# Loading the decay vector by rows and starting the r and k loads behind it: the prologue of a recurrent-attention plus ELU feed-forward kernel

## The chip, the cores and the metric

The kernel runs on one core of one Trainium2 chip. The metric is device time in microseconds (us) of one execution; lower is better. A profile of one execution on the same chip shows what each engine did. The engines are TensorE (PE, its weight loads PEld), VectorE (DVE), ScalarE (ACT), GpSimd (POOL), and SyncE (SP), which issues nearly all loads.

## The reference

Inputs are `r`, `k`, `v` of shape (4, 8, 768, 48) (batch B, heads H, steps S, head size D), the decay `w` and the bonus `u` of shape (8, 48), and two weight matrices of 384x2048 and 2048x384. All are float32.

```python
def _attn_ref(r, k, v, w, u):
    state = np.zeros((B, H, D, D)); y = np.zeros_like(r)
    for t in range(S):
        kt, vt, rt = k[:, :, t], v[:, :, t], r[:, :, t]
        cur = np.einsum('bhd,bhe->bhde', u[None] * kt, vt)
        y[:, :, t] = np.einsum('bhd,bhde->bhe', rt, state + cur)
        state = w[None, :, :, None] * state + np.einsum('bhd,bhe->bhde', kt, vt)
    return y

def _moe_ref(x, w_in, w_out):
    h = x @ w_in
    g = np.where(h > 0.0, h, np.exp(np.minimum(h, 0.0)) - 1.0)
    return g @ w_out
```

The attention output, turned to (3072, 384), goes through the feed-forward layer.

## The kernel before

The 768 steps are cut into six chunks of 128; a unit is one chunk of one batch, so there are 24 units. In a unit, r and k are turned by TensorE (products with the identity, `turn_in`, written `Tr` and `Tk` in the order), scaled by powers of w (`decay_r`, `decay_k`: `dr`, `dk`), multiplied with each other (`scores`: `A`), masked, and multiplied with v. The feed-forward weights are split into a high and a low part, and each layer product is made of three products. In the steady part TensorE goes through hidden and output products of 16 slices of the feed-forward layer per chunk, with the attention of later units put between.

The powers of w are good in this form only when every w lies between 0.8 and 1.2. So the program makes a flag, every engine reads it (`values_load`, L1122) and branches (`tc.If`, L1123) either to the fast path (`arm(general=False)`, the one that runs with these inputs) or to a general one. What comes ahead of the branch is `prepare` (L82 to L160).

In `prepare`, SP issues, in this order: w as one row of 384 on one partition (L89, for the test), w by channels into `w_col` (L94, two transfers in which every element lies by itself in memory), r of unit 0, u, k of unit 0, r and k of unit 1, v of unit 0. DVE takes minimum and maximum of the row (L122, L123) and makes the flag (L124, L126), and scans `w_col` four times to make the table of powers `pw` (L145). POOL makes the identity, clears the unused columns of the r, k and v tiles (`clear_pads`, L159), makes the mask and clears the states. PE runs seven float32 products of the identity with itself that nobody reads (`warm`, L497); each is two passes. `prepare` is written without an order: a scheduler puts each engine's instructions in a row.

Behind the branch the order is written out by hand (`tc.manual_schedule`), each engine going through it in its own program order. It begins `jk:8 inv Tr:0 dr:0 ub rua:0 rub:0 Lrk:2 Tk:0 ...`: eight more unread products with the identity (`keep_warm`, L502), the table of inverse powers on DVE (`inv`, L514 to L518), Tr and dr of unit 0 (L610, L670), u spread over the partitions (`ub`, a PE product at L506 and an ACT copy at L507), the products of r, k and u on POOL (`rua`, `rub`), the loads of unit 2, and Tk of unit 0. `Lw` are loads of feed-forward weights (L218, L221), `Lnk:0` (L171) the loads of r and k for the second chunk of batch 0.

Of the kernel before, what the change touches and what calls it, by code (L numbers as in the profile page):

```python
# [8 lines left out]
F32 = mybir.dt.float32  # L9
# [6 lines left out]
ALU = mybir.AluOpType  # L16
AX = mybir.AxisListType
PSUM = bass.MemoryType.PSUM

P = 128  # L20
B, H, S, D = 4, 8, 768, 48
DP = 64
HP = H // 2
DM, DFF = 384, 2048
# [6 lines left out]
ROWS = [slice(i * DP, i * DP + D) for i in range(2)]  # L31
# [1 line left out]
FILL = DP - D  # L33
Q = P // HP
W_LOW, W_HIGH = 0.8, 1.2
WARM = 7

DEEP, WIDE = 3, 2

START = """  # L40
jk:8 inv Tr:0 dr:0 ub rua:0 rub:0 Lrk:2 Tk:0 rua:1 rub:1 dk:0 sum:0 vd:0 Tr:1 zw dr:1 pr A:0 m0:0 Tk:1 Lrk:3 PT Lv:1
Tr:2 dk:1 kr:0 A:1 sum:1 m1:0 Lw:0 dr:2 Tk:2 d0a:1 m0:1 Y:0 ru:2 dk:2 Lv:2 Tk:3 d1a:1 m1:1 Tr:3 ru:3 xh:0 Y:1 sum:2
d1a:2 wd:0 xh:1 xl:0 dk:3 dr:3 kr:1 sum:3 d0:3 ma:0 Lw:3 Lw:4 A:2 d0a:2 xl:1 d1:3 S:0 sp:0 m1:2 Lv:3 m0:2 A:3 Lw:2
Lw:1 wd:2 S:1 m0:3 Y:2 Lnk:0 m1:3 rsd:0 xh:2 Lw:6 Y:3 xh:3 ma:2 sp:2 H:0 wdi:1 xl:2
# [28 lines left out]
class Kernel:  # L73
# [7 lines left out]
    def prepare(self, ctx):  # L81
        nc, tc = self.nc, self.tc  # L82
        cp = ctx.enter_context(tc.tile_pool(name="cp", bufs=1))

        self.rev = cp.tile([P, H, DP], F32, tag="rev", name="rev")
        self.state = [cp.tile([P, HP, 2 * D], F32, tag=f"state{b}", name=f"state{b}") for b in range(B)]
        early = self.rev.rearrange("p h d -> p (h d)")
        w_row = early[0:1, 0:DM]
        nc.sync.dma_start(w_row, self.w.rearrange("(o h) d -> o (h d)", o=1))  # L89

        w_col = cp.tile([P, HP], F32, tag="w_col", name="w_col")
        nc.vector.memset(w_col, 1.0)
        for i, rows in enumerate(ROWS):
            nc.sync.dma_start(w_col[rows, :], self.w[i::2, :].rearrange("a d -> d a"))  # L94

        self.slots = [
            (
                cp.tile([P, H, DP], F32, tag=f"r_t{i}", name=f"r_t{i}"),
                cp.tile([P, H, DP], F32, tag=f"k_t{i}", name=f"k_t{i}"),
                cp.tile([P, H, DP], F32, tag=f"v_t{i}", name=f"v_t{i}"),  # L100
            )
            for i in range(2)
        ]
        self.ident = cp.tile([P, P], F32, tag="ident", name="ident")
        make_identity(nc, self.ident)
        ones = early[:, DM:]
        nc.vector.memset(ones, 1.0)
        self.raw = {}
        for b in range(2):
            self.raw[0, b] = self.slots[b]  # L110
            self.clear_pads(self.slots[b])
        self.load_rk(0, 0, (0,))
        self.u_b = cp.tile([P, H, D], F32, tag="u_b", name="u_b")
        self.u_row, self.one = early[DP : DP + 1, 0:DM], ones[DP : DP + 1, :]
        nc.sync.dma_start(self.u_row, self.u.rearrange("(o h) d -> o (h d)", o=1))
        self.load_rk(0, 0, (1,))
        self.load_rk(0, 1)
        self.load_v(0, 0)


        lim = cp.tile([1, 4], F32, tag="lim", name="lim")
        nc.vector.tensor_reduce(lim[:, 0:1], w_row, axis=AX.X, op=ALU.min)  # L122
        nc.vector.tensor_reduce(lim[:, 1:2], w_row, axis=AX.X, op=ALU.max)  # L123
        nc.vector.tensor_single_scalar(out=lim[:, 2:3], in_=lim[:, 0:1], scalar=W_LOW, op=ALU.is_ge)  # L124
        self.flag = cp.tile([1, 1], I32, tag="flag", name="flag")
        nc.vector.scalar_tensor_tensor(  # L126
            self.flag, lim[:, 1:2], W_HIGH, lim[:, 2:3], op0=ALU.is_le, op1=ALU.mult
        )

        self.warm(WARM)  # L130


        self.mask = cp.tile([P, P], F32, tag="mask", name="mask")
        nc.gpsimd.memset(self.mask, 1.0)
        nc.gpsimd.affine_select(
            out=self.mask, in_=self.mask, pattern=[[1, P]], compare_op=ALU.is_gt,
            fill=0.0, base=0, channel_multiplier=-1,
        )
        for t in self.state:
            nc.gpsimd.memset(t, 0.0)  # L140
        self.pw = cp.tile([P, HP, P + 1], F32, tag="pw", name="pw")
        nc.vector.memset(self.pw[:, :, 0:1], 1.0)

        for a in range(HP):
            nc.vector.tensor_tensor_scan(  # L145
                self.pw[:, a, 1 : P + 1], w_col[:, a : a + 1].to_broadcast([P, P]), ones,
                1.0, op0=ALU.mult, op1=ALU.mult,
            )

        self.pairs = []  # L150
        for k in range(NF + 1):
            self.pairs.append([
                cp.tile([P, self.count(k), DM], F32R, tag=f"{n}{k}", name=f"{n}{k}")
                for n in ("wh", "wl")
            ])
# [333 lines left out]
                    self.done.add((name, m, b))  # L489
                    units[name](m, b)  # L490

    def warm(self, times):

        with self.tc.tile_pool(name="ps_w", bufs=1, space=PSUM) as ps:
            junk = ps.tile([P, P], F32, tag="junk", name="junk")
            for _ in range(times):
                self.nc.tensor.matmul(junk, lhsT=self.ident, rhs=self.ident, start=True, stop=True)  # L497

    def keep_warm(self, times):
        junk = self.ps.tile([P, T], F32, tag="h", name="junk", bufs=2)  # L500
# [615 lines left out]
@with_exitstack  # L1116
def rwkv_elu_ffn(ctx: ExitStack, tc: tile.TileContext, r, k, v, w, u, w_in, w_out, out):
    nc = tc.nc
    kn = Kernel(tc, r, k, v, w, u, w_in, w_out, out)
    kn.prepare(ctx)  # L1120

    near_one = nc.values_load(kn.flag, min_val=0, max_val=1)  # L1122
    with tc.If(near_one > 0) as cmp:  # L1123
        kn.arm(general=False)
    with cmp.Else():
        kn.arm(general=True)
# [30 lines left out]
```

## Time and profile before

| what | value |
|---|---|
| median of 3 runs | 495.19 us (494.24, 495.19, 496.57) |
| the profiled execution: its own time | 494.27 us |
| its span, first to last instruction | 492.5 us |
| PE busy | 483.7 us (98%) |
| DVE busy | 300.2 us (61%) |
| ACT busy | 244.6 us (50%) |
| POOL busy | 124.7 us (25%) |
| bytes moved by DMA | 49.13 MB |

Busy time counts instructions that compute; the unread products of the prologue count too. The end of a PE instruction is modelled, so rows of PE overlap a little. The 1.77 us between the execution's own time and its span lie outside the first and the last instruction.

### The profile page before, as it was taken

Reading aid. Unit: us, or ns where it says so; the run is one execution under the profiler, and the core shown is the slowest. Engines: PE = TensorE matmul, PEld = TensorE weight load, DVE = VectorE, ACT = ScalarE, POOL = GpSimd, SP = SyncE. Lnnn points to the kernel's source line nnn. Section 1 sums busy time; section 2 is a strip of 40 time slices with the busy share of each in tenths; the row PEclk is TensorE's granted clock in tenths of the full one; section 3 lists DMA queues with packets and bytes.
Section 4 is the critical chain, followed back from the end, with each engine's and each line's share of the span. In section 5 each row is a group of like instructions: output and inputs, shape, how many; then the busy total and the mean of one; then the engine's idle time right before and its main releaser. Section 6 shows DMA issues by size and latency. Waiting matters only on the chain.

```text
span 492.5 us, 12293 instructions
## 1 busy us (share of the span) xinstructions
PE 483.7 (98%) x5085; PEld 402.1 (82%) x5085; DVE 300.2 (61%) x514; ACT 244.6 (50%) x477; POOL 124.7 (25%) x156
## 2 busy tenths in 40 slices
PE   8999999999999999999999999999999999999995
PEld 7877887888888888888888888888888878889995
DVE  6989898955577647657457656475674443433332
ACT  3887776544435543544535435435444353344341
POOL 7766456451133231131220321301111000000000
PEclk9999999999999999999999999999999999999999
DMA  8899887561545461462431625514532000010002
GB/s 139 223 229 235 171 215 205 151 132 52 136 87 135 97 136 44 119 145 61 103 106 41 144 67 112 136 45 92 126 68 85 11 1 0 10 33 23 2 1 71
DMA packets 108454, 49.13 MB, mean 100 GB/s; under 512 B 89442, under 2 KB 104292, under 8 KB 108388
## 3 DMA queue, kind: packets, MB, share of 16 engines
q1 hardware_dynamic: 96580, 43.91, 39.1%
q10 hardware_dynamic: 11808, 4.33, 3.8%
q8 instruction: 42, 0.69, 0.6%
q14 instruction: 24, 0.20, 0.2%
HBM read 35.12 MB, written 13.11 MB: 98 GB/s over the span
## 4 chain that ended last, share of the span: by engine, by line
PE 85%; DVE 4%; DMA 3%; SPq 3%; ACT 2%; issue 1%; DVEq 0%; ACTq 0%
PE ps_acc L1080 38%; PE ps_h L1028 36%; PE ps_a L777 4%; PE ps_y L810 3%; DMA stage<-in_moe_w_in_dram 1%; PE ps_y L797 1%; DMA k_t<-in_k_dram 1%; SPq L171 1%; SPq L218 1%; PE ps_y L921 1%; PE ps_y L792 1%; DVE stage L562 1%; DMA stage<-in_moe_w_out_dram 1%; DVE wl L599 1%; DVE ps_h L1043 1%
## 5 line engine op out<-in xcount | busy, mean ns | idle before, releaser
L1028 PE MATMUL ps_h<-x,wh 128*128 128x512 f32 (+1 forms) x582 | 192.6, 388 | 0.9 <-DVE g L1051 0.6
L1080 PE MATMUL ps_acc<-g,wh 128*128 128x512 f32 x480 | 163.5, 396 | 0.1
L1043 DVE SCALAR_TENSOR_TENSOR ps_h<-g,ps_h 128x512 f32<-128x512 f32 x96 | 66.6, 694 | 126.0 <-ACT g L1038 125.9
L1028 PEld LDWEIGHTS ps_h<-x,wh 128*128 128x128 f32 x582 | 108.8, 188 | 24.7 <-DVE g L1051 1.8
L1037 ACT ACTIVATE g<-ps_h 128x512 f32<-128x512 f32 x96 | 57.3, 597 | 127.5 <-PE ps_h L1028 99.6
L1028 PE MATMUL ps_h<-x,wl 128*128 128x512 f32 (+1 forms) x291 | 112.7, 387 | 0.0
L1080 PEld LDWEIGHTS ps_acc<-g,wh 128*128 128x128 f32 x480 | 90.0, 188 | 20.9 <-issue 0.8
L1080 PE MATMUL ps_acc<-g,wl 128*128 128x512 f32 x240 | 93.7, 390 | 0.0
L1049 ACT ACTIVATE g<-ps_h 128x512 fp32r<-128x512 f32 x96 | 57.3, 597 | 70.0 <-DVE ps_h L1043 59.2
L1051 DVE SCALAR_TENSOR_TENSOR g<-ps_h,g 128x512 fp32r<-128x512 f32 x96 | 66.2, 690 | 41.8 <-ACT g L1049 37.2
L1028 PEld LDWEIGHTS ps_h<-x,wl 128*128 128x128 f32 x291 | 54.6, 188 | 10.9
L828 POOL TENSOR_TENSOR a<-ident,diag 128x512 f32<-128x512 f32 x22 | 24.3, 1106 | 152.3 <-PE ps_y L921 79.8
L1038 ACT ACTIVATE g<-g 128x512 f32<-128x512 f32 x96 | 60.7, 632 | 3.1
L1080 PEld LDWEIGHTS ps_acc<-g,wl 128*128 128x128 f32 x240 | 45.1, 188 | 8.7
L658 POOL TENSOR_TENSOR tb<-rk,qw 128x512 f32<-128x512 f32 x16 | 20.8, 1301 | 69.6 <-DMA rk<-blocks 69.6
L1080 PE MATMUL ps_acc<-wh,g 128*128 128x384 f32 x128 | 33.9, 336 | 0.0
L835 DVE COPY_PREDICATED a<-mask,ps_a 128x512 f32<-128x512 int32 x46 | 33.4, 734 | 0.2 <-ACT a L824 0.2
L824 ACT ACTIVATE a<-ident,diag 128x128 f32<-128x128 f32 x96 | 30.4, 391 | 0.4 <-DVE diag L715 0.4
L1080 PEld LDWEIGHTS ps_acc<-wh,g 128*128 128x128 f32 x128 | 23.2, 188 | 0.4 <-DVE g L1051 0.2
L946 ACT CAST x<-ps_y 128x256 fp32r<-128x256 f32 (+1 forms) x40 | 10.8, 322 | 22.8 <-DVE state L936 21.0
L1080 PE MATMUL ps_acc<-wl,g 128*128 128x384 f32 x64 | 21.4, 335 | 0.0
L732 POOL TENSOR_TENSOR sw<-state,pw 48x192 f32<-48x192 f32 x30 | 18.2, 607 | 7.4 <-DVE state L936 6.3
(111 smaller groups left out, 442.6 us busy)
## 6 DMA issues: line engine op xcount, KB each, us to landing
blocks<-tb SPq DMA_DIRECT2D x64, 128.0 KB, 2.4
rk<-blocks SPq DMA_DIRECT2D x16, 512.0 KB, 3.5
stage<-in_moe_w_out_dram SPq DMA_DIRECT2D x16, 383.8 KB, 4.6
stage<-in_moe_w_in_dram SPq DMA_DIRECT2D x64, 95.8 KB, 3.9
out_dram<-stage ACTq DMA_DIRECT2D x80, 48.0 KB, 1.7
r_t<-in_r_dram SPq DMA_DIRECT2D x17, 192.0 KB, 4.4
k_t<-in_k_dram SPq DMA_DIRECT2D x17, 192.0 KB, 5.0
v_t<-in_v_dram SPq DMA_DIRECT2D x17, 192.0 KB, 5.4
```

The costliest lines, as they stand in the source:

```text
L658: (self.nc.gpsimd if i else self.nc.vector).tensor_mul(dst, src, by)
L777: nc.tensor.matmul(un["pa"][i][keys, a * P : (a + 1) * P], lhsT=un["k"][rows, a, keys], rhs=un["r"][rows, a, :], start=True, stop=True, sk ...
L824: self.nc.scalar.activation(un["a"][i][:, a, :], self.ident, AF.Copy, scale=diag[:, a : a + 1])
L828: self.nc.gpsimd.tensor_mul(un["a"][i], self.ident.unsqueeze(1).to_broadcast([P, HP, P]), diag.unsqueeze(2).to_broadcast([P, HP, P]),)
L835: self.nc.vector.copy_predicated(un["a"][i], self.mask.bitcast(I32).unsqueeze(1).to_broadcast([P, HP, P]), un["pa"][i].rearrange("p (a t) ...
L1028: self.nc.tensor.matmul(ph[:, part], lhsT=a[:, c * P : (c + 1) * P], rhs=x[:, c, part], start=(c == 0 and i == 0), stop=(c == NC - 1 and i ...
L1037: nc.scalar.activation(g, ph, AF.Relu, scale=-1.0)
L1038: nc.scalar.activation(g, g, AF.Exp, scale=-1.0)
L1043: self.nc.vector.scalar_tensor_tensor(ph, g, -1.0, ph, op0=ALU.add, op1=ALU.max)
L1049: nc.scalar.activation(part, g, AF.Copy, scale=W_SCALE)
L1051: nc.vector.scalar_tensor_tensor(part, g, W_SCALE, self.g[n, f][2].bitcast(F32), op0=ALU.mult, op1=ALU.subtract)
L1080: self.nc.tensor.matmul(at, lhsT=lhs, rhs=rhs, start=(f == 0 and i == 0), stop=(f == NF - 1 and i == 2),)
```

## The change

w is loaded once, as 8 rows of 48 on 8 partitions. Its form by channels is made on PE by two small products of those rows with columns of the identity, and copied to `w_col` by DVE. The test is made on the 8 rows: DVE marks the elements that lie in range and takes the minimum by row, a PE product with ones adds the 8 rows, and DVE turns the sum into the flag. The loads of r and k of unit 0 are issued right behind w, u behind them. The unread products ahead of the branch are six instead of seven and use a tile of ones instead of the identity: two ahead of the small products, one behind them, three behind the sum. ACT makes one early copy of one element. The unread products behind the branch are four instead of eight. `prepare` now runs in the order in which it is written (`tc.manual_schedule`).

```diff
-WARM = 7
+WARM, WARM_AHEAD = 6, 2
 START = """
-jk:8 inv Tr:0 dr:0 ub rua:0 rub:0 Lrk:2 Tk:0 ...
+jk:4 inv Tr:0 dr:0 ub rua:0 rub:0 Lrk:2 Tk:0 ...
@@ prepare
-        w_row = early[0:1, 0:DM]
-        nc.sync.dma_start(w_row, self.w.rearrange("(o h) d -> o (h d)", o=1))
+        w_rows, ones = early[0:H, 0:D], early[:, DM:]
+        nc.sync.dma_start(w_rows, self.w)
         w_col = cp.tile([P, HP], F32, tag="w_col", name="w_col")
+        nc.vector.memset(ones, 1.0)
         nc.vector.memset(w_col, 1.0)
-        for i, rows in enumerate(ROWS):
-            nc.sync.dma_start(w_col[rows, :], self.w[i::2, :].rearrange("a d -> d a"))
...
-        self.ident = cp.tile([P, P], F32, tag="ident", name="ident")
-        make_identity(nc, self.ident)
-        ones = early[:, DM:]
-        nc.vector.memset(ones, 1.0)
-        self.raw = {}
-        for b in range(2):
-            self.raw[0, b] = self.slots[b]
-            self.clear_pads(self.slots[b])
-        self.load_rk(0, 0, (0,))
+        self.raw = {(0, b): self.slots[b] for b in range(2)}
+        self.load_rk(0, 0)
...
         nc.sync.dma_start(self.u_row, self.u.rearrange("(o h) d -> o (h d)", o=1))
-        self.load_rk(0, 0, (1,))
         self.load_rk(0, 1)
         self.load_v(0, 0)
-        lim = cp.tile([1, 4], F32, tag="lim", name="lim")
-        nc.vector.tensor_reduce(lim[:, 0:1], w_row, axis=AX.X, op=ALU.min)
-        nc.vector.tensor_reduce(lim[:, 1:2], w_row, axis=AX.X, op=ALU.max)
-        nc.vector.tensor_single_scalar(out=lim[:, 2:3], in_=lim[:, 0:1], scalar=W_LOW, op=ALU.is_ge)
+        self.ident = cp.tile([P, P], F32, tag="ident", name="ident")
+        make_identity(nc, self.ident)
+        for b in range(2):
+            self.clear_pads(self.slots[b])
+        lim = cp.tile([H, D + 2], F32, tag="lim", name="lim")
+        ok, all_ok, junk_a = lim[:, 0:D], lim[:, D : D + 1], lim[0:1, D + 1 : D + 2]
+        nc.scalar.copy(junk_a, ones[0:1, 0:1])
+        self.pw = cp.tile([P, HP, P + 1], F32, tag="pw", name="pw")
+        nc.vector.memset(self.pw[:, :, 0:1], 1.0)
         self.flag = cp.tile([1, 1], I32, tag="flag", name="flag")
-        nc.vector.scalar_tensor_tensor(
-            self.flag, lim[:, 1:2], W_HIGH, lim[:, 2:3], op0=ALU.is_le, op1=ALU.mult
-        )
-        self.warm(WARM)
+        with tc.tile_pool(name="ps_w", bufs=1, space=PSUM) as ps:
+            junk = ps.tile([P, P], F32, tag="junk", name="junk")
+            pc = ps.tile([P, HP], F32, tag="pc", name="ps_w")
+            rows_ok = ps.tile([1, 1], F32, tag="rows_ok", name="rows_ok")
+            self.warm(junk, ones, WARM_AHEAD)
+            for i, rows in enumerate(ROWS):
+                nc.tensor.matmul(
+                    pc[rows, :], lhsT=w_rows, rhs=self.ident[0:H, i:H:2],
+                    start=True, stop=True, skip_group_check=True,
+                )
+            nc.vector.tensor_single_scalar(out=ok, in_=w_rows, scalar=W_LOW, op=ALU.is_ge)
+            nc.vector.scalar_tensor_tensor(ok, w_rows, W_HIGH, ok, op0=ALU.is_le, op1=ALU.mult)
+            nc.vector.tensor_reduce(all_ok, ok, axis=AX.X, op=ALU.min)
+            self.warm(junk, ones, 1)
+            nc.tensor.matmul(rows_ok, lhsT=all_ok, rhs=ones[0:H, 0:1], start=True, stop=True)
+            self.warm(junk, ones, WARM - WARM_AHEAD - 1)
+            for rows in ROWS:
+                nc.vector.tensor_copy(w_col[rows, :], pc[rows, :])
+            nc.vector.scalar_tensor_tensor(
+                self.flag, rows_ok, H - 0.5, ones[0:1, 0:1], op0=ALU.is_ge, op1=ALU.mult
+            )
...
-    def warm(self, times):
-        with self.tc.tile_pool(name="ps_w", bufs=1, space=PSUM) as ps:
-            junk = ps.tile([P, P], F32, tag="junk", name="junk")
-            for _ in range(times):
-                self.nc.tensor.matmul(junk, lhsT=self.ident, rhs=self.ident, start=True, stop=True)
+    def warm(self, junk, t, times):
+        for _ in range(times):
+            self.nc.tensor.matmul(junk, lhsT=t, rhs=t, start=True, stop=True)
@@ rwkv_elu_ffn
-    kn.prepare(ctx)
+    with tc.manual_schedule():
+        kn.prepare(ctx)
```

## Rows read from the trace of the kernel before

**Rows 1.** The page: busy time of each engine, share of the span, instructions.

```profile
PE 483.7 (98%) x5085; PEld 402.1 (82%) x5085; DVE 300.2 (61%) x514; ACT 244.6 (50%) x477; POOL 124.7 (25%) x156
```

**Rows 2.** Windows: stretch and length, busy us by engine, PEclk, DMA share, GB/s.

```profile
20.00:30.00 10.00, 9.42 (x177) 7.75 (x173) 8.78 (x16) 7.39 (x15) 4.42 (x6) 1.00 0.83 208
30.00:80.00 50.00, 49.65 (x543) 40.17 (x544) 46.05 (x72) 38.40 (x71) 31.75 (x35) 1.00 0.93 214
80.00:488.00 408.00, 406.82 (x4137) 339.08 (x4135) 229.75 (x392) 188.30 (x367) 72.36 (x82) 1.00 0.35 80
```

**Rows 3.** Chain that ended last, 0 to 50 us: start, length, what.

```profile
0.80 0.35 SPq L89
...
17.52 3.90 DMA stage<-in_moe_w_in_dram
...
22.71 5.98 DMA k_t<-in_k_dram
```

**Rows 4.** Waits of PE, 0 to 60 us: total, times, longest.

```profile
PE ps_kT L610 <- DMA k_t<-in_k_dram: 0.3, 1, 0.3
```

**Rows 5.** Timeline of SP: start, length, line, transfer, count.

```profile
1.21 0.84 SPq L94 DMA_DIRECT2D w_col<-in_w_dram  x2
2.09 0.45 SPq L171 DMA_DIRECT2D r_t<-in_r_dram  x1
2.58 0.44 SPq L115 DMA_DIRECT2D rev<-in_u_dram  x1
3.06 0.39 SPq L171 DMA_DIRECT2D k_t<-in_k_dram  x1
...
7.08 0.37 SPq L171 DMA_DIRECT2D raw<-in_r_dram  x1
```

**Rows 6.** Line L171, 0 to 30 us: from issue to landing.

```profile
DMA to landing us min/median/max: 3.1/3.8/6.0
```

**Rows 7.** Timeline of DVE, ACT and POOL ahead of 8 us, in brackets the idle time before.

```profile
0.93 0.17 DVE L107 MEMSET rev<- 128x128 f32 x1
...
2.11 0.54 DVE L122 TENSOR_REDUCE lim<-rev 1x1 f32<-1x384 f32 x1 [1.00 <-DMA rev<-in_w_dram]
...
3.60 0.43 DVE L145 TENSOR_TENSOR_SCAN pw<-w_col,rev 128x128 f32<-128x128 f32 x1 [0.43 <-DMA w_col<-in_w_dram]
3.94 0.12 DVE L126 SCALAR_TENSOR_TENSOR flag<-lim 1x1 int32<-1x1 f32 x1
3.99 1.03 DVE L145 TENSOR_TENSOR_SCAN pw<-w_col,rev 128x128 f32<-128x128 f32 x3
...
4.71 1.28 ACT L507 ACT_TABLE_LOAD   x1 [4.71 <-DVE flag L126]
4.77 0.94 POOL L159 MEMSET raw<- 128x128 f32 x6 [0.73 <-DVE flag L126]
...
5.13 0.55 DVE L514 RECIPROCAL near<-pw 128x64 f32<-128x64 f32 x1
...
7.55 0.69 DVE L670 TENSOR_TENSOR rk<-ps_rT,pw 128x512 f32<-128x512 f32 x1 [0.72 <-PE ps_rT L610]
```

**Rows 8.** Timeline of PE ahead of 9 us.

```profile
1.53 3.35 PE L497 MATMUL junk<-ident 128*128 128x128 f32 x14 [1.53 <-POOL ident masks.py:199]
5.03 1.94 PE L502 MATMUL junk<-ident 128*128 128x128 f32 x8
6.76 0.75 PE L610 MATMUL ps_rT<-ident,r_t 128*128 128x128 f32 x4
7.45 0.91 PE L506 MATMUL ps_u<-rev 1*128 1x384 f32 x2
8.28 0.66 PE L610 MATMUL ps_kT<-ident,k_t 128*128 128x128 f32 x4
8.78 0.60 PE L610 MATMUL ps_rT<-ident,r_t 128*128 128x128 f32 x4
```

**Rows 9.** Timeline of PE, a single pass of `keep_warm`.

```profile
6.55 0.42 PE L502 MATMUL junk<-ident 128*128 128x128 f32 x1
```

More of the change, by code (lines that the diff above doesn't have):

```diff
@@ L35 @@
 W_LOW, W_HIGH = 0.8, 1.2
-WARM = 7
+WARM, WARM_AHEAD = 6, 2
 DEEP, WIDE = 3, 2
 START = """
-jk:8 inv Tr:0 dr:0 ub rua:0 rub:0 Lrk:2 Tk:0 rua:1 rub:1 dk:0 sum:0 vd:0 Tr:1 zw dr:1 pr A:0 m0:0 Tk:1 Lrk:3 PT Lv:1
+jk:4 inv Tr:0 dr:0 ub rua:0 rub:0 Lrk:2 Tk:0 rua:1 rub:1 dk:0 sum:0 vd:0 Tr:1 zw dr:1 pr A:0 m0:0 Tk:1 Lrk:3 PT Lv:1
 Tr:2 dk:1 kr:0 A:1 sum:1 m1:0 Lw:0 dr:2 Tk:2 d0a:1 m0:1 Y:0 ru:2 dk:2 Lv:2 Tk:3 d1a:1 m1:1 Tr:3 ru:3 xh:0 Y:1 sum:2
@@ L140, in prepare @@
             nc.gpsimd.memset(t, 0.0)
-        self.pw = cp.tile([P, HP, P + 1], F32, tag="pw", name="pw")
-        nc.vector.memset(self.pw[:, :, 0:1], 1.0)
         for a in range(HP):
```

## The prediction

> **What bounds the kernel now.** I read the page's busy times first. PE is busy 483.7 of 492.5 us [rows 1], so a change in the prologue can only win what PE does not need: idle time, and the unread products. Next the windows. From 80 us to the last product PE is busy 406.82 of 408 us [rows 2]: that stretch has no room and moves as a block, by whatever the work ahead of it gains. From 20 to 30 us PE is busy only 9.42 of 10 us with the DMA engines at 0.83 of their time, and from 30 to 80 us 49.65 of 50 [rows 2]. So the question is what sets the time at which PE leaves the first 30 us. The chain of work answers it: it begins with SP's first issue at 0.80 us, stays on SP's issues and on landings of loads, and comes to the load of k for the second chunk, issued at 22.71 us and landed 5.98 us later, at 28.69 [rows 3]. In PE's waits that landing is the end of 0.3 us of idle time [rows 4]. The reader is to see two chains running side by side, the stream of loads and PE's own list, with the stream last by 0.3 us. A gain in the prologue is kept only if both move.
>
> **The stream of loads.** r of unit 0, the first large load, is issued at 2.09 us. Ahead of it stand the two w_col transfers, issued from 1.21 us on [rows 5]. They go away, so r is issued at 1.21: 0.88 earlier. k comes at 1.21 + 0.45 + 0.04 = 1.70 instead of 3.06, u at 1.70 + 0.39 + 0.04 = 2.13 instead of 2.58, and what comes behind, 0.88 earlier than now [rows 5]. w as 8 rows is one transfer like w as one row, and I leave its issue at 0.35 [rows 3]; with w_col's 0.42 each [rows 5] it could be 0.1 more. I take it that the queue stays full from then on, as a landing of 5.98 us at 22.71 speaks for [rows 3], and let the whole stream, k at 28.69 included, move by 0.88. Bounds: nothing, if what holds the stream is not its start, and 1.2 if the small packets of w_col also held r back.
>
> **The flag.** Now: w is there at 2.11, the flag is written from 3.94 to 4.06, behind two reductions and the first scan, which waited for w_col until 3.60 [rows 7]. After: three DVE steps on 8x48 elements, one reduction among them. Their prices are not in the trace; the nearest are 0.12 for a tiny one and 0.54 for a reduction over 384 elements [rows 7], so from 0.36 to 0.78 together; I take 0.45, nearer to the tiny ones since each has 48 elements per partition. That makes 2.56. Meanwhile PE has begun at 1.10, when the ones are set [rows 7], not at 1.53. One pass of 128 columns starts every 0.216 us now (eight from 5.03 to 6.76) [rows 8], so the first two products, four passes, are through at 1.96; the two small products wait for w at 2.11, the filler takes 0.43, and the sum over rows starts between 2.6 and 2.9. A pass takes 0.42 from start to end [rows 9]; with DVE's 0.12 the flag is there at 3.2 to 3.45. I take 3.4, 0.66 earlier. The small products, two passes each with 4 columns, cost between nothing and four full passes (0.86); I take 0.1.
>
> What is queued behind the new waits: on PE the fillers and the branch; on DVE, behind the flag, the four scans. These took 0.43 + 1.03 = 1.46 [rows 7], so they end at 4.9 instead of 5.02, and the inverse table, 1.7 us from 5.13 on, at 6.7. dr of unit 0 then starts at 6.7, not 7.55 [rows 7]; the product that needs it comes only after dk, which waits for PE. The two w_col copies and the later scans thus cost nothing, under a cover of more than 1 us. ACT's early copy pulls the 1.28 us table load out of a time in which ACT idles 4.71 us [rows 7]: nothing.
>
> The price of w's landing: the row shows 0.80 to 2.11, 1.31 us [rows 3, 7]. The Trainium skill (DMA: Bandwidth & Descriptors, Anatomy of one DMA) states about 2.0 us of fixed cost per DMA, for transfers issued from GpSimd. By it w lands at 2.8, the flag at 4.1 and unit 0 on PE 0.5 later than below, and the sum would be a gain of about 0.7 instead of 0.88; the measurement decides, so I keep 1.31.
>
> **PE's list.** PE is not at full speed yet in this stretch. Passes start every 0.216 us in the unread products and every 0.125 us from 8.28 on (four to 8.78); the four of Tr:0 take 0.69, two at each pace [rows 8]. Those paces are the two levels, 1.2 and 2.4 GHz, and the rise lies at about 7.2 us, after unbroken products since 1.53. Now the unread products stop starting at 1.53 + 14 x 0.216 = 4.55 and the eight begin at 5.03, 0.97 behind the flag [rows 7, 8]. After: the last six passes end at about 4.1, the flag plus 0.97 is 4.37, the passes plus the same gap of 0.48 make 4.6. I take 4.6, then four passes: Tr:0 starts at 5.45 instead of 6.76. r must be there: 1.21 plus 3.1 (the shortest landing) is 4.3, plus 3.8 (the median) 5.0 [rows 6]; at 6.0 it would be 7.2, a delay for which nothing in an empty queue speaks.
>
> How much of the 1.3 us is real work? If the rise stays at 7.2, PE does (7.2 - 5.45)/2 = 0.87 us worth of full-speed work by then, against 0.22 now. So PE's list is 0.65 ahead. With the 0.3 by which PE waits today, it could use up to 0.96 of the stream's lead, and the stream gives 0.88. Sum: the smaller, 0.88 us, against the profiled execution's 494.27: 493.39. The median of the runs lies 0.92 above that execution, so the median should come to 495.19 - 0.88 = 494.3 us.
>
> **Rivals.**
>
> *The rise comes later.* The PE stretch ahead of the branch now has holes (the wait for w, the wait for DVE) and fewer products. With the rise at R, PE's lead is 4.26 - R/2: 0 at 8.5, and the whole gain is gone at 9.1, where the lead is -0.3. It decides from 7.4 on. Typical price: gain 0.3, 494.9; at R = 11, 0.9 lost, 496.1. For: the products are fewer. Against: PE starts 0.43 earlier, and the holes are short. The Trainium skill (TensorE: Matmul & The Clock Gate, Part 1) says that the clock is released by sustained activity and that the moment differs by about 500 ns between runs; half a microsecond later would make the gain 0.7. No row of a single execution can show that spread.
>
> *The stream does not move.* If landings are set by the rate at which the DMA engines work off the queue and not by its start, k still lands at 28.69, and PE, 0.65 ahead on its list, only waits longer for it: no gain from the lead, at most some hundredths behind that wait, so 495.2. For: the DMA share of 0.83 [rows 2]. Against: a full queue that starts earlier also ends earlier.
>
> *More.* The small packets of w_col stood ahead of r in the same queue; with them gone the stream moves 1.2, and if the rise also comes earlier PE follows: gain 1.3, 493.9.
>
> *Slower: the pads.* In the written order `clear_pads` comes behind the loads of the same tiles. If POOL has to wait for these loads, the last of the pads falls behind a load issued ahead of 7.08 - 0.88 = 6.2, so at some 6.2 + 3.1 = 9.3 [rows 5, 6]; the 0.94 of further pads [rows 7] come behind it, and the loads of unit 2 behind those, at over 10 instead of 6.2. Some 3 to 4 us of stream are lost: 498.5. It decides if a strided pad counts as touching the loaded columns. Against: the ones were set at 0.93, into the tile into which w was still being loaded until 2.11 [rows 7], so writes to different parts of a tile pass each other.
>
> **How the numbers follow.** Chances: forecast 0.58, rise later 0.18, stream not moved 0.11, more 0.07, pads 0.06. The forecast's bounds (0.5 to 1.2) give 494.0 to 494.7. The three runs of before lie from 0.95 below to 1.38 above their median, and a new median can fall anywhere in much of that. Together with the late rise at the top and the larger gain at the bottom the range is 492.9 to 496.3. A measurement of this kernel tells 0.5%, 2.5 us, from no change. Only a gain that no row shows would pass that bound, 0.05; only the pads or a very late rise would on the other side, 0.06; so 0.89 for no difference.
>
> **What would show it.** Right: r issued at about 1.2, flag at about 3.4, the first Tr at about 5.5 with starts 0.216 apart, Tk of unit 0 about 0.65 ahead of 8.28, k's landing near 27.8 with PE waiting for it, and everything behind 30 us shifted by one constant near 0.9. Wrong: pads on POOL behind a DMA wait; a pace of 0.216 still at 8 us; k's landing still near 28.7; or a new PE wait between 30 and 80 us that takes the lead back.

## The result, and the profile after

The change made the kernel slower: 498.02 us (22 runs, 496.38 to 501.20) against 495.70 (22 runs), ratio 1.0051 [1.0038, 1.0065]. The forecast was 494.3 us, with a range that ended at 496.3. The profiled execution took 496.42 us; its span is 494.7, 2.2 us longer than before's.

The steps of the prologue came nearly as planned. SP's timeline after (start, length, line, transfer):

```profile
0.80 0.41 SPq L89 DMA_DIRECT2D rev<-in_w_dram  x1
1.27 0.41 SPq L180 DMA_DIRECT2D r_t<-in_r_dram  x1
1.73 0.56 SPq L180 DMA_DIRECT2D k_t<-in_k_dram  x1
...
6.19 0.37 SPq L180 DMA_DIRECT2D raw<-in_r_dram  x1
...
18.06 0.43 SPq L184 DMA_DIRECT2D raw<-in_v_dram  x1
18.84 4.71 SPq L227 DMA_DIRECT2D stage<-in_moe_w_in_dram  x4
...
24.64 0.52 SPq L180 DMA_DIRECT2D k_t<-in_k_dram  x1
```

Against [rows 5], r is issued 0.82 earlier and the first load of unit 2 still 0.89 earlier (6.19, not 7.08). Then the lead is lost. SP's timeline before, for the two issues that answer to 18.06 and 18.84:

```profile
18.00 0.43 SPq L175 DMA_DIRECT2D raw<-in_v_dram  x1
18.47 3.15 SPq L218 DMA_DIRECT2D stage<-in_moe_w_in_dram  x4
```

At 18 us nothing is left of the lead; k for the second chunk is issued at 24.64, 1.93 later than in [rows 3]. The windows show where it went: before first, then after (stretch and length, busy us of PE, PEld, DVE, ACT, POOL, PEclk, DMA share, GB/s). The DMA share adds up the times of all packets, and packets overlap, so it can exceed 1.

```profile
8.00:10.00 2.00, 1.65 (x14) 1.14 (x14) 0.94 (x2) 1.61 (x2) 0.99 (x2) 1.00 1.44 185
10.00:12.00 2.00, 2.00 (x27) 1.88 (x26) 1.95 (x4) 0.82 (x3) 1.92 (x3) 1.00 1.07 214
12.00:14.00 2.00, 1.80 (x23) 1.40 (x21) 2.00 (x4) 1.64 (x5) 2.00 (x4) 1.00 1.01 215
```

```profile
8.00:10.00 2.00, 1.66 (x19) 1.42 (x20) 1.19 (x3) 1.96 (x3) 1.34 (x2) 1.00 1.49 163
10.00:12.00 2.00, 2.00 (x22) 1.64 (x20) 2.00 (x5) 0.77 (x2) 1.92 (x3) 1.00 1.50 163
12.00:14.00 2.00, 1.81 (x24) 1.48 (x28) 1.85 (x5) 1.69 (x6) 2.00 (x3) 1.00 1.51 169
20.00:30.00 10.00, 7.46 (x133) 6.33 (x130) 8.59 (x15) 7.75 (x18) 1.82 (x4) 1.00 0.89 172
30.00:80.00 50.00, 49.30 (x578) 40.11 (x576) 45.36 (x73) 38.27 (x72) 31.52 (x33) 1.00 0.95 220
80.00:488.00 408.00, 406.83 (x4136) 339.34 (x4135) 233.11 (x393) 188.86 (x368) 74.32 (x85) 1.00 0.38 79
```

The loads run at 163 GB/s with a DMA share of 1.50 where before they rose to 214 at 1.07: fewer bytes, more time in packets. PE pays at 20 to 30 us: busy 7.46 instead of 9.42 [rows 2], 1.96 of the 2.2 us; 0.35 more goes between 30 and 80; from 80 us on nothing changes. After's chain of work runs through that stretch on loads and on the queue behind them (start, length, what):

```profile
11.30 4.87 DMA stage<-in_moe_w_in_dram
...
16.19 1.34 SPq L227
...
17.57 5.77 DMA stage<-in_moe_w_in_dram
```

where the transfer at 17.52 took 3.90 before [rows 3]. PE's waits after, 0 to 100 us (total, times, longest): of these the last alone names a load. The others come by way of ACT, whose L559 waited 1.36 us for the load into `stage` at 18.93, and DVE behind it.

```profile
PE ps_st L927 <- DVE x L904: 1.2, 1, 1.2
...
PE ps_y L816 <- PE ps_st L927: 0.7, 1, 0.7
PE ps_y L816 <- DVE wl L605: 0.6, 1, 0.6
...
PE ps_kT L616 <- DMA k_t<-in_k_dram: 0.3, 1, 0.3
```

The 0.3 of [rows 4] is still there, two microseconds later:

```profile
30.77 0.63 PE L616 MATMUL ps_kT<-ident,k_t 128*128 128x128 f32 x4 [0.32 <-DMA k_t<-in_k_dram]
```

### The profile page after: what moved, and what is told of

It is laid out like the page before. It is cut to its first block, busy times and chain, and to the rows that moved or that the text cites. A ratio compares the mean times of both kernels' runs of the same rounds, so it can differ in the third digit from the quotient of the medians.

```text
span 494.7 us, 12296 instructions
## 1 busy us (share of the span) xinstructions
PE 483.4 (98%) x5085; PEld 401.9 (81%) x5085; DVE 302.9 (61%) x516; ACT 245.1 (50%) x478; POOL 124.2 (25%) x156
## 4 chain that ended last, share of the span: by engine, by line
PE 89%; DMA 3%; SPq 2%; DVE 2%; ACT 2%; issue 1%; ACTq 0%; POOL 0%; DVEq 0%; POOLq 0%
PE ps_acc L1086 39%; PE ps_h L1034 37%; PE ps_a L783 4%; PE ps_y L816 4%; DMA stage<-in_moe_w_in_dram 3%; PE ps_y L803 1%; PE ps_y L927 1%; PE ps_y L798 1%; SPq L227 1%; SPq L180 1%; DVE ps_h L1049 0%; PE junk L503 0%; ACT g L1044 0%; ACT g L1043 0%; ACTq L1119 0%
```

## The experiments

The expectations call theories by letters and say what each means; a batch is a set of kernels run on one chip beside the kernel before. Ratios are to that. The edits are shown abridged.

**First batch: which edit slows the loads?** e1 puts u back between r and k, e2 issues two transfers of the old `w_col` form again (into an unread tile), e4 goes back to eight unread products; e3 is the kernel before with only the order of r, k and u of the change.

```diff
e1 (after):  self.load_rk(0, 0, (0,)); u; self.load_rk(0, 0, (1,))
e2 (after):  + w_idle = cp.tile(...); + 2 x dma_start(w_idle[rows], w[i::2].rearrange("a d -> d a"))
e4 (after):  -jk:4 ...   +jk:8 ...
e3 (before): -load_rk(0, 0, (0,)); u; load_rk(0, 0, (1,))   +load_rk(0, 0); u
```

> The changed kernel with one edit undone: u is issued between r and k of unit 0 again. Theory A (the pace of the loads): in the changed kernel the loads run at some 163 GB/s from 5 to 14 us where before they ran above 200 from 10 us on, and it is r and k back to back that brings them there; then this run has the pace of before from 10 us on and a ratio to the kernel before near 0.999. Theory B (the pace is set by the start without the two w_col transfers): this run stays at 163 GB/s until about 14 us, ratio near 1.005. Theory C (the prologue on PE costs the time, not the loads): also near 1.005, whatever the pace.

> The changed kernel with the two element-wise transfers of w issued behind w again, into a tile that nobody reads; all else as changed, the stream of r and k starts at about 2.1 us again. Theory A (r and k back to back): still 163 GB/s until about 14 us, ratio near 1.005 or above. Theory B (the start without these transfers): the pace of before, above 200 GB/s from 10 us on, ratio near 1.000. Theory C (PE's prologue): ratio near 1.005 with the loads at the pace of before.

> The kernel before with one edit of the change: r and k of unit 0 issued back to back, u behind them; w_col transfers, flag, unread products and order as before. Theory A: the pace falls to 163 GB/s until about 14 us and the ratio is near 1.005. Theories B and C: no change, ratio 0.999 to 1.001.

> The changed kernel with eight unread products behind the branch instead of four. Theories A and B: PE starts some 0.5 to 0.8 us later on unit 0 but waits for the loads anyway: ratio 1.004 to 1.006, the pace of the loads unchanged. Theory C (too few products, the loss is on PE): ratio near 1.001.

Measured: e1 1.0069 [1.0043, 1.0095], e2 1.0105 [1.0078, 1.0131], e4 1.0070 [1.0052, 1.0089], e3 1.0006 [0.9987, 1.0025]. All three made from after stay at 163 to 168 GB/s up to 14 us; e3 has before's pace (219 GB/s at 10 to 12 us). So none of these edits is the cause: not the load order (theory A), not the missing small transfers (theory B), not the smaller number of unread products behind the branch (theory C, as far as e4 tests it).

**Second batch: the place of the tiles.** What no view of the profile shows is in the program: where the tiles lie. `cp` puts tiles one behind another, each rounded up to 32 bytes. The change makes `lim` 200 bytes per partition instead of 16, so everything behind it (`mask`, the tables, `stage`, the r, k, v tiles of units 2 and 3, called `raw`) moves by 192 bytes. In r, k and v tiles a head has 48 numbers, 192 bytes, and heads start 256 bytes apart. A tile that starts at a multiple of 256, or up to 64 behind it, keeps each 192-byte row between two multiples; one that starts at 160, 192 or 224 has every row cross one. From the programs' placement (bytes modulo 256), with the profile's GB/s at 10 to 12 us and the ratio:

```
kernel                           r_t0, k_t0..  stage  raw   GB/s 10-12   ratio
before                              160          0      0      214       1
after                               160        192    192      163       1.0051
e2 after, w_col transfers           192        224    224      164       1.0105
f1 before, lim of 200 bytes         160        192    192      163       1.0077
f2 after, lim of 288 bytes          160          0      0      224       1.0001
f5 before, lim of 64 bytes          160         32     32      190       1.0031
f3, g1 after, all on 256              0          0      0   219, 226     0.9997, 1.0010
f4, g2 before, all on 256             0          0      0   221, 220     0.9983, 0.9975
```

Theory D: it is this placement. Theory E, the rival: it is something that the changed prologue does (the order of the engines, ACT's early copy, w as rows). f1 is the test, an edit that computes nothing:

```diff
f1 (before): -lim = cp.tile([1, 4], ...)          +lim = cp.tile([1, 50], ...)
f5 (before):                                      +lim = cp.tile([1, 16], ...)
f2 (after):  -lim = cp.tile([H, D + 2], ...)      +lim = cp.tile([H, 72], ...)
f3 (after):  +lim = cp.tile([H, 112], ...)        +w_col = cp.tile([P, 32], ...)[:, 0:HP]
```

> The kernel before, with the tile lim made 50 columns wide instead of 4, and nothing else: no instruction changes, but each tile placed behind it moves by 192 bytes per partition, as in the changed kernel. Theory D (placement: in the raw tiles of units 2 and 3 the 192 bytes of a head then run across a multiple of 256 bytes, and such loads go at the slow pace): 163 GB/s until about 14 us, ratio 1.004 to 1.007. Rival E (the written order of the prologue, the early ACT copy or the load of w as 8 rows sets the pace): no change, ratio 0.999 to 1.001, above 200 GB/s from 10 us on.

> The changed kernel with lim 72 columns wide instead of 50 (the rest of it unused), which puts the raw tiles and all behind at a multiple of 256 bytes again. Theory D: above 200 GB/s from about 9 us on, and the 0.4 to 0.9 us that the new prologue gains on PE and the loads come through: ratio 0.998 to 0.9995. Rival E: 163 GB/s until 14 us, ratio 1.004 to 1.007.

> The changed kernel with w_col and lim made wider so that the r, k and v tiles of units 0 and 1 too begin at a multiple of 256 bytes, and the raw tiles as well. Theory D: no stretch at 163 GB/s in the first 14 us, loads of 196 KB landing some 0.7 instead of 1.2 us apart, ratio 0.994 to 0.998. Rival E: the slow pace stays, ratio 1.004 to 1.007.

> The kernel before with lim 16 columns wide: the raw tiles and all behind lie 32 bytes past a multiple of 256, where 192 bytes still end ahead of the next multiple of 256 but begin at no multiple of 64. Theory D as stated (running across a multiple of 256 is what counts): the pace of before, ratio 0.999 to 1.001. Theory D in another form (any start off a multiple of 64 or 128 is slow): 163 GB/s until 14 us, ratio 1.004 or above.

Measured: f1 1.0077 [1.0049, 1.0105], f2 1.0001 [0.9978, 1.0025], f3 0.9997 [0.9974, 1.0020], f5 1.0031 [1.0011, 1.0052]. E falls: f1 has the old prologue and after's loads. In f1 the granted clock fell as well: it is 0.53 from 23 to 30 us of its profile, behind a stretch from 20 to 23 us in which PE was busy 1.29 of 3.0, and the mean granted clock of its seven runs is 0.990 to 0.996, where f4's twelve have 0.997 to 1.000. So part of its ratio may be the clock, as a consequence of the wait. Its windows:

```profile
8.00:10.00 2.00, 1.66 (x18) 1.42 (x20) 1.01 (x2) 1.98 (x3) 1.35 (x2) 1.00 1.47 163
10.00:12.00 2.00, 1.90 (x22) 1.57 (x18) 2.00 (x5) 0.82 (x2) 1.92 (x3) 1.00 1.50 163
...
20.00:30.00 10.00, 6.49 (x116) 5.42 (x115) 7.34 (x13) 6.20 (x15) 1.08 (x2) 0.67 0.94 177
```

and f3's, with the changed prologue:

```profile
10.00:12.00 2.00, 1.91 (x20) 1.54 (x20) 2.00 (x5) 0.77 (x2) 1.92 (x3) 1.00 1.09 219
...
20.00:30.00 10.00, 9.69 (x172) 8.16 (x169) 9.23 (x17) 8.02 (x16) 4.95 (x6) 1.00 0.76 212
```

So the pace of the loads came back as theory D had it. The gain that it forecast for f2 and f3 (ratios up to 0.9995 and 0.998) does not show in their medians, though both intervals reach into it, and its forecast for f5 (0.999 to 1.001) missed, since it had left out the weight rows. The tiles that the engines read have moved too, but from 80 to 488 us PE gets through as many products in f1 (4135) and after (4136) as in before (4137), so it is not the engines' own work that became slower.

f5 divides the matter by tile. The DMA view, 4 to 24 us (issues of a tile, count, size, median us from issue to landing), before, then f1, then f5:

```profile
stage<-in_moe_w_in_dram SPq DMA_DIRECT2D x12, 95.8 KB, 3.9
...
raw<-in_r_dram SPq DMA_DIRECT2D x2, 192.0 KB, 3.6
```

```profile
stage<-in_moe_w_in_dram SPq DMA_DIRECT2D x12, 95.8 KB, 5.0
...
raw<-in_r_dram SPq DMA_DIRECT2D x2, 192.0 KB, 4.8
```

```profile
stage<-in_moe_w_in_dram SPq DMA_DIRECT2D x13, 95.8 KB, 4.9
...
raw<-in_r_dram SPq DMA_DIRECT2D x2, 192.0 KB, 3.6
```

At 32 behind a multiple the r rows cross nothing and land in 3.6 us as before; the long weight rows, which no longer start on a multiple, take 4.9. In the packet records the median 192-byte packet takes 15 ns in the quick stretches and 27 to 28 in the slow ones. Before shows both in one execution: r, k and v of units 0 and 1, at 160, go at 170 GB/s from 6 to 8 us, and the `raw` tiles, at 0, at 214 from 10 on. Crossing alone is not the whole of it, though: the same tiles at 160 still load at 230 GB/s from 5 to 6 us, with a DMA share of 1.21. What brings the lower rate on was not settled. The Trainium skill (DMA: Bandwidth & Descriptors, How a descriptor splits into AXI transactions) states that a transaction must start at an address that is a multiple of 256 bytes, and that the first one of a row which does not start there begins at the multiple below it. By this a row that runs across one multiple more takes one transaction more. This agrees with f1 and f5; the page speaks of reading, and the runs moved only the side in SBUF that is written.

**Third and fourth batch: what is the changed prologue worth on equal placement?** f4 puts before's tiles on 256. f6 is f3 with more fillers (8, three of them ahead of the small products), f7 is f3 with eight unread products, g1 and g2 are f3 and f4 once more, side by side, and g3 is g2 with e3's order.

```diff
f4 (before): +w_col = cp.tile([P, 32], ...)[:, 0:HP]   +lim = cp.tile([1, 48], ...)
f6 (f3):     -WARM, WARM_AHEAD = 6, 2   +WARM, WARM_AHEAD = 8, 3
f7 (f3):     -jk:4 ...                  +jk:8 ...
g3 (f4):     -load_rk(0, 0, (0,)); u; load_rk(0, 0, (1,))   +load_rk(0, 0); u
```

> The kernel before with w_col and lim made wider, so that the r, k and v tiles of units 0 and 1 as well as the raw tiles begin at a multiple of 256 bytes; its prologue is untouched. Theory D: the stretch at 165 GB/s from 6 to 9.5 us goes, the clock level rises as before; ratio 0.994 to 0.999, and equal or below that of the changed kernel placed in the same way (0.9997), if the changed prologue's fewer products cost as much as its earlier start gives.

> The changed kernel with all tiles placed at multiples of 256 bytes, and with eight unread products ahead of the branch, three of them ahead of the small products, so that PE has hardly a hole from 1.1 to 5.2 us. Theory F (in the changed prologue the holes let the clock level rise only at 14 us in some executions, which eats the gain): the rise stays ahead of 8 us and the ratio is 0.994 to 0.998, below the 0.9997 without these products. Rival G (the rise is not what eats it): 0.999 to 1.001.

> The changed kernel with all tiles placed at multiples of 256 bytes and eight unread products behind the branch instead of four. Theory F: the rise is ahead of 8 us more often, against 0.4 to 0.8 us of later start; ratio 0.996 to 0.999. Rival G: 0.9997 plus the later start, 1.000 to 1.002.

> The changed kernel with its loads' destinations on multiples of 256 bytes (the same kernel as f3), now beside the old prologue in the same placement on one chip. Theory G (the new prologue as such costs PE its early rise of the clock, so what it wins in loading it gives back): the rise at 6.5 us or later in this profile, the first intra product (L756) at 9.1 us or later, and a time 0.1 to 0.3 per cent above that of g2, 495.2 to 495.8 us. Rival H (f3 and f4 differed only because they ran on two chips): equal to g2 within 0.05 per cent. Rival I (the prediction's 0.88 us is there once the placement is equal): 0.1 to 0.2 per cent below g2.

> The kernel before with the same placement (the same kernel as f4). Theory G: the rise at 4.9 to 5.4 us, the first intra product (L750) near 8.9 us, a time of 0.9975 to 0.999 of the kernel before. Rival H: the rise at any moment from 4.9 to 7.5 us, and no time that differs from g1's.

> g2 with the first two loads of r and k one behind the other and u behind them (e3's order on aligned tiles). If the earlier start of the loads is worth anything once they run at the full rate: up to 0.5 us below g2, with k of the first slot landing 0.5 us earlier; if PE's own chain of fillers, transposes and products sets the start, as theory G has it: equal to g2 within 0.1 per cent.

Measured: f4 0.9983 [0.9969, 0.9998], f6 1.0031 [1.0011, 1.0050], f7 1.0023 [1.0006, 1.0041]; then g1 1.0010 [0.9992, 1.0028], g2 0.9975 [0.9958, 0.9991], g3 0.9971 [0.9952, 0.9990]. The chip is not it (theory H): on one chip the changed prologue is 0.35% (1.6 us) slower than the old one with the same placement, so theory I falls as well. f6's cure missed both of its bands, and g3 says that the order of the loads is worth nothing there.

What differs in these profiles is when PE's pace rises from 0.216 us per pass to 0.125. The windows do not show this first rise (PEclk reads 1.00 ahead of it too), so it is read from the starts of the passes, and to the tenth from the trace's records of the granted clock. The sixteen products of the first `scores` show it: they take 1.16 us at the quicker pace and 2.03 to 2.08 at the slower. In the nine profiles of the old prologue they start between 8.72 and 9.89 us and all take 1.16; in the eleven of the changed one they start between 9.16 and 10.76, and in four of them (e1, f2, g1 and h2 below) they still run at the slower pace. Nor did every old profile rise early: in g2 itself the pace was still slow at 6.76, where theory G had the rise at 4.9 to 5.4, and they start at 9.89. With one profile of each run, four of eleven against none of nine can still be chance.

**Fifth batch: which part delays the rise?** h1 puts the fillers of ones into the old prologue, h2 puts the identity back into those of the changed one, h3 takes four of the unread products out of the old one, and h4 gives h2 eight of them. All on 256.

```diff
h1 (f4): -matmul(junk, lhsT=self.ident, rhs=self.ident, ...)   +lhsT=self.ones, rhs=self.ones
h2 (f3): -self.warm(junk, ones, ...)                           +self.warm(junk, self.ident, ...)
h3 (f4): -jk:8 ...   +jk:4 ...
h4 (h2): -jk:4 ...   +jk:8 ...
```

> The old prologue on aligned tiles with one part of the change alone: its fourteen warming passes multiply the tile of ones (from 1.1 us) and not the identity (from 1.5 us). Theory J (the fillers of ones are why the clock rises late in the changed prologue): the rise at 6.5 us or later and 0.2 to 0.4 per cent slower than the same prologue with the identity, 495 to 496 us, ratio 0.999 to 1.002. Theory K (it is the breaks which the small products of w and of the flag put between the fillers, or the order of the engines' work): no change, ratio 0.9965 to 0.9985, 493.5 to 494.3 us.

> The changed prologue on aligned tiles with its warming passes on the identity again. Theory J: the rise at 5 to 7 us, a time like that of the old prologue on aligned tiles or up to 0.5 us below it, ratio 0.9965 to 0.9985. Theory K: 495.2 to 495.8 us, ratio 0.9995 to 1.002, as with the ones.

> The old prologue on aligned tiles with four identity products in place of eight ahead of the first transposes, another part of the change alone. Theory J, and K too: no change beyond 0.3 us (the transposes wait for r or for the fillers either way), ratio 0.997 to 0.9985. If the number of these products is what the early rise needs: 0.2 to 0.4 per cent slower, ratio 0.999 to 1.002.

> The changed prologue on aligned tiles with both the identity in its warming passes and eight identity products, so that only its loads of w, its small products, its flag and its order differ from the old one. Theory J: 0.2 us above h2 at most, ratio 0.997 to 0.999. Theory K: as the changed prologue with the ones and eight products (f7), ratio 1.001 to 1.003.

Measured: h1 0.9978 [0.9958, 0.9997], h2 0.9999 [0.9972, 1.0026], h3 1.0025 [1.0001, 1.0048], h4 1.0007 [0.9984, 1.0029]. J falls: ones cost the old prologue nothing, and the identity does not cure the changed one. h2's timeline of PE shows the late rise:

```profile
5.42 1.09 PE L508 MATMUL junk<-ident 128*128 128x128 f32 x4
6.30 1.06 PE L616 MATMUL ps_rT<-ident,r_t 128*128 128x128 f32 x4
7.29 1.64 PE L512 MATMUL ps_u<-rev 1*128 1x384 f32 x2
...
10.76 2.08 PE L756 MATMUL ps_a<-rk 48*128 48x128 f32 x16
12.77 0.66 PE L616 MATMUL ps_kT<-ident,k_t 128*128 128x128 f32 x4
```

PE computes without a break there and keeps the slower pace to 12.7 us. h2's twelve times fall into two groups, 492.6 to 493.9 and 496.2 to 497.6 (g1's into 493.6 to 495.1 and 496.2 to 496.8); its profiled execution, the one with this rise, took 496.2. So the changed prologue can be as quick as the old one on equal placement (g2: 492.8 to 494.8), or 3 us slower. That the second group is the late rise is argued from that execution and from g1's (late rise, 496.8), not shown for the others.

h3 has another story, told by its waits of PE (0 to 80 us):

```profile
PE ps_y L810 <- DMA raw<-in_v_dram: 2.3, 1, 2.3
...
PE ps_a L750 <- DVE rk L670: 0.9, 1, 0.9
```

Four unread products fewer and an early rise brought Tr of unit 0 to 5.55, and PE then waited 0.9 for DVE and 2.3 for v. Why it ends slower than with eight was not settled. It matters for the changed prologue, which has four as well: this part of the change alone, with an early rise, costs the old prologue some 0.4% (1.0025 against 0.9983 and 0.9975 of f4 and g2). Against it as the cause there: with eight, f7 (1.0023) and h4 (1.0007) are no faster than with four.

## Why the prediction was wrong

**The loads' start: right.** r at 1.27 (1.21), the first load of unit 2 0.89 ahead (0.88). w by rows took 0.41 to issue, not 0.35.

**The failed step** stands in the part on the stream of loads: "I take it that the queue stays full from then on", and then "let the whole stream, k at 28.69 included, move by 0.88". The queue stayed full, but its rate fell from 214 to 163 GB/s. k landed 6.0 us after its issue at 24.64, and PE's product that waited for it began at 30.77; the forecast had the landing at 27.8. The lower rate came from `lim`, a tile of the test, by the place of the tiles behind it (f1: 1.0077 with nothing else changed; f2 and f3: loads at 224 and 219 GB/s, 1.0001 and 0.9997). The working asked of each edit what it executes and not what it allocates; neither the forecast nor a rival had this. Even the rival "The stream does not move" kept the rate. (In f1's 20 to 30 us PEclk is 0.67, which after's is not, so what f1's profile takes more than after's need not be loads.) Whether the forecast's 0.88 us would have come with before's placement stays open: f2 is that case, and its interval, 0.9978 to 1.0025, holds both the forecast's 0.9982 and no change.

**The flag: a size off.** Timeline of DVE after:

```profile
2.21 0.22 DVE L132 TENSOR_SCALAR lim<-rev 8x48 f32<-8x48 f32 x1 [1.12 <-DMA rev<-in_w_dram]
...
3.52 0.14 DVE L140 SCALAR_TENSOR_TENSOR flag<-rows_ok,rev 1x1 int32<-1x1 f32 x1 [0.39 <-PE rows_ok L136]
3.59 1.35 DVE L154 TENSOR_TENSOR_SCAN pw<-w_col,rev 128x128 f32<-128x128 f32 x4
...
5.85 1.74 DVE L524 TENSOR_TENSOR qw<-near 128x128 f32<-128x128 f32 x4
7.51 0.68 DVE L676 TENSOR_TENSOR rk<-ps_rT,pw 128x512 f32<-128x512 f32 x1
```

The three steps on 8x48 run from 2.21 to 2.88, 0.67 against the 0.45 taken (bounds 0.36 to 0.78); the flag is written at 3.66, not 3.4. w was there at 2.21, 1.41 after its issue (1.31 taken). The four products of the inverse table now take 1.74 us (0.90 before), beside a product of POOL that starts at 5.84. In the runs of both prologues where that product starts at 6.6 or later they take 0.90 (e2: 6.75), where it starts between 5.4 and 6.3, 1.26 to 1.74. The cover of more than 1 us which the working named for them is gone with that, since dr of unit 0 follows right behind them at 7.51.

**PE's list: right in kind, too large.** Timeline of PE after:

```profile
1.12 1.22 PE L503 MATMUL junk<-rev 128*128 128x128 f32 x4 [1.12 <-DVE pw L120]
...
3.30 0.18 PE L136 MATMUL rows_ok<-rev,lim 8*1 8x1 f32 x2
3.41 1.65 PE L503 MATMUL junk<-rev 128*128 128x128 f32 x6
5.17 1.09 PE L508 MATMUL junk<-ident 128*128 128x128 f32 x4
6.05 1.06 PE L616 MATMUL ps_rT<-ident,r_t 128*128 128x128 f32 x4
...
7.93 0.66 PE L616 MATMUL ps_kT<-ident,k_t 128*128 128x128 f32 x4
...
9.37 1.16 PE L756 MATMUL ps_a<-rk 48*128 48x128 f32 x16 [0.34 <-DVE rk L676]
```

The sum over rows started at 3.30 (2.6 to 2.9 forecast), so the last fillers end at 5.06 and not at 4.1; the unread products begin at 5.17 (4.6), Tr of unit 0 at 6.05 (5.45), Tk 0.35 ahead of [rows 8] (0.65). The pace rose near 7.2, as assumed.

**The rivals.** "The pads" did not come: POOL's first pads ran from 1.31 to 2.24 without a wait. "The rise comes later" was not this profile's case, but it is real: in four of eleven profiles of the changed prologue the pace rises between 12.5 and 15.0 us, where the rival went to 11. On aligned tiles the changed prologue loses 1.6 us (g1 against g2) where the forecast gave it 0.88, and the late rise is one difference of this size that the profiles show; that it is the whole of the 1.6 us is not shown, since h3 loses as much with an early rise. What in the prologue makes a late rise likelier stays open: ones instead of the identity are excluded by h1 and h2, the load order by e1, which has the old order and rises last of all (15.0 us); the breaks by the small products and the written order were not tried alone.

**The best version** is the old prologue on aligned tiles: f4 and g2, 0.9983 [0.9969, 0.9998] and 0.9975 [0.9958, 0.9991], are 1.0 to 1.4 us better than before. Of the tiles that are loaded early only r, k and v of units 0 and 1 lie differently there (160 before, 0 now), which speaks for the same cause. g3, 0.9971 [0.9952, 0.9990], is the same within its interval.

## What to carry to other kernels

When an edit changes the size of any tile, look where the tiles behind it have moved before blaming what it executes: 184 bytes more in a tile of a test cost this kernel 0.5%, and the windows' DMA share (1.50 at 163 GB/s, against 1.07 at 214) tells it apart from a late start. Place tiles that short rows are loaded into so that no row crosses a multiple of 256 bytes; a neutral padding of a small tile is the cheapest test. And a lead of a microsecond in a prologue is only worth what PE's pace leaves of it, so look at the rise in several executions.

## What the runs showed of the hardware

In a full queue (10 to 12 us) rows of 192 bytes that cross a multiple of 256 bytes in SBUF load at 163 to 164 GB/s (after, e1, e2, e4, f1), others at 207 to 226 (the runs with all tiles on 256). Weight rows that start 32 bytes behind a multiple land in 4.9 us (f5), not 3.9 (before), in the median. Four products of DVE take 1.26 to 1.74 us beside a product of POOL, 0.90 without it. The rise of PE's pace from 1.2 to 2.4 GHz came between 4.4 us (f5) and 15.0 us (e1) in kernels that feed PE with nearly unbroken products from 1.1 to 1.5 us on. The Trainium skill (TensorE: Matmul & The Clock Gate, Part 1) gives about 500 ns of spread between runs; the profiles here show far more, also between two of the same kernel: 6.7 and 12.5 us (f3, g1), 4.9 and 7.4 us (f4, g2).
